# Second product's results added to the rows by accumulating transfers issued from GpSimd, in seven of eight blocks

## The chip, the cores and the metric

The kernel runs on one NeuronCore of a Trainium2 chip. The metric is the device time of one execution in microseconds (us), the median over runs. A core has a matrix engine (TensorE, PE in the profile), three other compute engines (VectorE = DVE, ScalarE = ACT, GpSimd = POOL), a queue engine (SyncE = SP) that issues most transfers, and 16 DMA engines that carry them. Each engine works through its own queue in order and waits on semaphores for the others.

## The reference

```python
def _attn_ref(q, k, v, omega):            # (8, 8, 576, 64), omega (128, 64)
    ...
    q_p, k_p = (phi(q_s), phi(k_s))       # exp features, 128 per head
    kv = np.einsum('bhsm,bhsd->bhmd', k_p, v)
    z = np.sum(k_p, axis=2)
    num = np.einsum('bhsm,bhmd->bhsd', q_p, kv)
    den = np.einsum('bhsm,bhm->bhs', q_p, z)[..., None] + 1e-06
    return (num / den).astype(np.float32)

def _moe_ref(x, w_ch1, w_ch2):            # x: (8, 576, 512), weights 512x2048 and 2048x512
    X = np.fft.fft(x, axis=1)
    X = np.fft.fft(X, axis=2)
    u = x + np.real(X).astype(np.float32)
    mu = np.mean(u, axis=-1, keepdims=True)
    var = np.mean((u - mu) ** 2, axis=-1, keepdims=True)
    un = (u - mu) / np.sqrt(var + 1e-06)
    ch = np.maximum(un @ w_ch1, 0.0) @ w_ch2
    return (u + ch).astype(np.float32)
```

`reference` runs the first, puts its heads side by side (8 x 576 rows of 512), and runs the second on that. All in float32.

## The kernel before

There are 8 x 576 = 4608 rows of 512. A first stage (to about 424 us) computes attention and the Fourier mix and writes the rows `u` to DRAM (`us`); it also does the two-layer network for the first 512 rows in a plain way. The second stage takes the other 4096 rows in eight blocks of 512 (`NTB` = 8, `j` = 0 to 7). This is where the change lies.

In each block both matrix products of the network are done by a fast scheme: each operand is cut into 2 x 2 parts, seven products of sums of parts are formed instead of eight, and the results are added together.

- **First product**, `first_of(j, fc)`: eight chunks `fc` of the hidden width. TensorE multiplies (L1310), ScalarE and VectorE evict with the relu into `hid` (L1296, L1324, L1362), and GpSimd forms four sums of parts per chunk, into `hs` and `hid` (L1377).
- **Second product**, `product_of(j, i, cells)`: seven products in the order 1, 2, 4, 5, 6, 7, 3 (`ORDER`). Products 1, 2, 4 and 7 read `hid`; 5, 6 and 3 read `hs`. Each product is itself done by the same scheme, as seven *leaves* of four matmuls (L1490). A leaf reads one tile `wl` of the second weight, 256 KB, loaded by SyncE from DRAM (L1393) into one of 12 buffers. Sums of the left factor come from VectorE (L1457). The leaves are evicted by ScalarE to `s` (L1465) and by VectorE with an add into `part` (L1470: c11, c12, c22); the last leaf's quarter is copied into `part` by ScalarE (L1523).

`part` holds one product's result: 128 partitions of 2 x 256 floats, 256 KB. There are four such buffers. The block's rows are in two cells `cells[0]` and `cells[1]` (tiles `ur2`, three buffers, loaded from `us`, L948), each of two row tiles of 512 columns; `cell(t, m)` is the half `m` of the columns of cell `t`. Each product's `part` is added into one or two of these halves: product 1 into (0,0), 2 into (0,0), 4 into (1,0), 5 into (0,1) and (1,1), 6 into (0,1), 7 into (1,1) and (1,0), 3 into (0,1). Before 6 and 7 add, the `part` of 6 and then that of 7 are added to the kept `part` of product 1 (`cells["u"]`), and that buffer is what is added; it is released after product 7, the others after their own last add. The function `plus` makes such an add, on GpSimd or VectorE, whichever would end earlier by the planner (L1530). When all adds of a cell are done, SyncE stores it (`stored`, L954).

The order of everything is set when the program is built: the class `Listing` takes streams of `Step`s, each with an engine, an assumed duration, the events it waits for and the buffers it takes and gives, and always issues the step that could begin first by its own clock. In the second stage there is no list of fixed picks, so a change of any step's assumed cost can move the order on every engine. Each engine then runs its list in order; tile dependences become semaphore waits.

The last product of the last block has its own ending (`ends`).

Of the kernel before, what the change touches and what calls it, by code (L numbers as in the profile page):

```python
# [15 lines left out]
ALU = mybir.AluOpType  # L16
# [19 lines left out]
PE, ACT, DVE, POOL, SP, NONE = "pe", "act", "dve", "pool", "sp", "none"  # L36
# [244 lines left out]
def kernel(  # L281
# [10 lines left out]
    nc = tc.nc  # L292
# [30 lines left out]
    NTB = (B * S - NPLAIN * TP) // TB  # L323
# [152 lines left out]
    us = dram.tile([B * S, DM], F32, name="us")  # L476
# [954 lines left out]
    def product_of(j, i, cells):  # L1431
# [10 lines left out]
        part = late.tile([128, 2, HM], F32, name="part", tag="part", bufs=4)  # L1442
# [83 lines left out]
        def plus(o, other, **kw):  # L1526
            step = Step({POOL: 1.35, DVE: 0.7}, port=True, **kw, bias=0.06)
            yield step
            eng = nc.gpsimd if step.eng == POOL else nc.vector
            eng.tensor_tensor(out=o, in0=o, in1=other, op=ALU.add)  # L1530

        def cell(t, m):
            return cells[t][:, :, HM * m : HM * m + HM]

        def done(n):
            return (("second", j, n), "done")

        us = tuple(("ur2", j, t) for t in range(2))
        if i in (1, 6, 7):
# [4 lines left out]
            part, give = cells["u"], ("part",) if i == 7 else ()  # L1544
        else:
            to = {2: ((0, 0),), 4: ((1, 0),), 5: ((0, 1), (1, 1)), 3: ((0, 1),)}[i]
            give = ("part",)
        for n, (t, m) in enumerate(to):
            last = n == len(to) - 1
            yield from plus(  # L1550
                cell(t, m), part[:], after=(us[t],), give=give if last else (),
                makes=done(i) if last else None,
            )

    def second_of(j, cells):
        t0 = (NPLAIN * TP + TB * j) // 128
# [25 lines left out]
    def halves():  # L1582
        for j in range(NTB):
            for fc in range(HF):
                yield Step(NONE, take=("set", "ht", "ht"))
                yield Fork(first_of(j, fc))
            cells = {}
            yield Fork(second_of(j, cells))
            for i in ORDER:
                yield Step(NONE, take=("set",))  # L1590
                yield Fork(product_of(j, i, cells))
# [40 lines left out]
```

## Time and profile before

| | |
|---|---|
| median of 3 runs | 1170.17 us (1165.61 to 1170.54) |
| profiled execution, from first to last instruction | 1172.2 us |
| granted TensorE clock, mean | 0.996 of full speed |
| second stage | from 424 us to the end |
| L1470 in the second stage (VectorE) | 168 instructions, 49.0 us |
| L1523 in the second stage (ScalarE) | 55 instructions, 15.3 us |
| L1530 into the cells, on VectorE | 39 instructions, 26.8 us |
| L1530 into the kept `part`, on VectorE | 16 instructions, 11.0 us |
| DMA queue of SyncE | 166576 packets, 218.09 MB |

How to read it: the profile is of one execution, which took 1172.2 us; all durations are from it. Busy time is the time in which an engine executed; instructions that only issue a transfer or wait are not counted. A row of a group reads: line, engine, operation, output <- inputs, count, then busy time and mean duration in ns, then the idle time of the engine just before these instructions and what ended it. The chain of waits is followed back from the last instruction: each piece is either work on an engine, or the time from the issue of a transfer to its arrival. In tables of stretches, each engine's busy time stands with its instruction count, then the granted TensorE clock, the busy share of the 16 DMA engines, and GB/s.

### The profile page before, as it was taken

How to read it: one execution, taken by the hardware profiler on the slowest of the kernel's cores; microseconds unless marked ns; L12 is line 12 of the kernel's file. 1: busy time of each engine (PE TensorE's matmuls, PEld its weight loads, DVE VectorE, ACT ScalarE, POOL GpSimd, SP SyncE). 2: the span in 40 equal slices, each digit the busy share in tenths (PEclk: the TensorE clock that was granted, in tenths of full speed). 3: DMA queues.
4: the chain of work that ended last, by engine and by line, in shares of the span. 5: the costliest groups of instructions: out<-in, count | busy, mean ns of one | idle time of the engine just before them, and what ended most of it. 6: DMA issues, size and time to landing. Idle time of an engine off the chain costs nothing.

```text
span 1172.2 us, 31328 instructions
## 1 busy us (share of the span) xinstructions
PE 1153.5 (98%) x12437; PEld 1032.9 (88%) x12437; DVE 754.7 (64%) x1573; ACT 436.8 (37%) x1485; POOL 430.4 (37%) x496
## 2 busy tenths in 40 slices
PE   8999999999999999999999999999999999999998
PEld 7888888779777868998998998898999899899898
DVE  5999999986676655744754664573573574474255
ACT  6998898866444212122112212212212212221211
POOL 2433444455472106225225324413513512522421
PEclk8999999999999999999999999999999999999999
DMA  7866765665662254873783593694495396388055
GB/s 218 224 188 186 240 181 178 203 210 163 207 196 101 77 162 139 263 264 85 222 278 112 172 308 99 152 317 141 112 319 190 82 290 231 83 258 263 35 166 203
DMA packets 167217, 220.34 MB, mean 188 GB/s; under 512 B 50080, under 2 KB 81056, under 8 KB 167072
## 3 DMA queue, kind: packets, MB, share of 16 engines
q1 hardware_dynamic: 166576, 218.09, 60.7%
q8 instruction: 98, 1.61, 0.6%
q14 instruction: 47, 0.39, 0.1%
q10 hardware_dynamic: 496, 0.26, 0.1%
HBM read 179.24 MB, written 43.25 MB: 190 GB/s over the span
## 4 chain that ended last, share of the span: by engine, by line
PE 88%; DMA 5%; DVE 4%; ACT 2%; SPq 1%; issue 1%; DVEq 0%
PE banks L1310 33%; PE banks L1490 27%; PE banks L1099 5%; PE banks L606 5%; PE banks L1122 4%; PE banks L512 4%; DMA wl<-w2l 3%; PE banks L640 2%; PE banks L687 2%; PE banks L849 2%; PE banks L799 1%; ACT e L566 1%; DVE nmx L549 1%; DMA kq<-in_k_dram 1%; PE banks L809 1%; PE banks L860 1%
## 5 line engine op out<-in xcount | busy, mean ns | idle before, releaser
L1490 PE MATMUL banks<-wl,sums 128*128 128x128 f32 x1792 | 217.4, 275 | 0.0
L1490 PEld LDWEIGHTS banks<-wl,sums 128*128 128x128 f32 x1792 | 208.6, 192 | 0.0
L1296 DVE CUSTOM_DVE_ANT_0 hid<-banks,s 128x256 f32<-128x256 f32 x192 | 80.9, 424 | 188.8 <-PE banks L1310 188.8
L566 ACT ACTIVATE e<-banks,nmx 128x128 f32<-128x128 f32 x576 | 165.3, 434 | 23.2 <-DVE nmx L549 22.4
L1324 ACT ACTIVATE s<-banks 128x256 f32<-128x256 f32 x192 | 73.7, 384 | 259.0 <-PE banks L1310 259.0
L1310 PE MATMUL banks<-unT,w 128*128 128x256 f32 x704 | 166.3, 379 | 0.0
L1310 PEld LDWEIGHTS banks<-unT,w 128*128 128x128 f32 x704 | 133.2, 190 | 18.3 <-issue 0.5
L1530 POOL TENSOR_TENSOR ur<-ur,part 128x512 f32<-128x512 f32 x32 | 47.3, 1479 | 267.1 <-ACT part L1523 187.0
L1465 ACT ACTIVATE s<-banks 128x128 f32<-128x128 f32 x168 | 46.6, 278 | 256.7 <-PE banks L1490 220.3
L1310 PE MATMUL banks<-tt,w1s 128*128 128x256 f32 x512 | 126.3, 379 | 0.0
L1310 PEld LDWEIGHTS banks<-tt,w1s 128*128 128x128 f32 x512 | 97.0, 190 | 13.7 <-DVE hid L1296 0.4
L1490 PE MATMUL banks<-wl,hid 128*128 128x128 f32 x768 | 100.0, 276 | 3.2 <-DMA wl<-w2l 3.1
L1470 DVE TENSOR_TENSOR part<-banks,s 128x128 f32<-128x128 f32 x168 | 49.0, 292 | 83.4 <-PE banks L1490 82.2
L549 DVE TENSOR_REDUCE nmx<-banks 128x8 f32<-128x1024 f32 (+1 forms) x96 | 89.3, 951 | 19.7 <-PE banks L606 15.5
L1490 PEld LDWEIGHTS banks<-wl,hid 128*128 128x128 f32 x768 | 94.0, 192 | 6.0 <-DMA wl<-w2l 4.5
L606 PE MATMUL banks<-om,kqT 64*64 64x128 f32 (+1 forms) x2088 | 80.6, 278 | 1.9 <-ACT kv L656 1.2
L1310 PE MATMUL banks<-unT,w1s 128*128 128x256 f32 x320 | 79.5, 379 | 0.0
L606 PEld LDWEIGHTS banks<-om,kqT 64*64 64x64 f32 (+1 forms) x2088 | 65.8, 140 | 13.3 <-issue 4.3
L1490 PE MATMUL banks<-wl,hs 128*128 128x128 f32 x576 | 75.1, 275 | 0.5 <-DVE part L1470 0.4
L1490 PEld LDWEIGHTS banks<-wl,hs 128*128 128x128 f32 x576 | 70.1, 192 | 1.2 <-DVE part L1470 0.6
L1377 POOL TENSOR_TENSOR hs<-hid,hs 128x256 f32<-128x256 f32 x64 | 50.1, 784 | 57.2 <-issue 37.1
L1310 PEld LDWEIGHTS banks<-unT,w1s 128*128 128x128 f32 x320 | 60.4, 190 | 8.7
(128 smaller groups left out, 1914.6 us busy)
## 6 DMA issues: line engine op xcount, KB each, us to landing
wl<-w2l SPq DMA_DIRECT2D x392, 256.0 KB
raw<-in_moe_w_ch_dram SPq DMA_DIRECT2D x32, 512.0 KB
kq<-in_k_dram SPq DMA_DIRECT2D x32, 288.0 KB
kq<-in_q_dram SPq DMA_DIRECT2D x32, 288.0 KB
vd<-in_v_dram SPq DMA_DIRECT2D x32, 288.0 KB
u<-us SPq DMA_DIRECT2D x36, 256.0 KB
ur<-us SPq DMA_DIRECT2D x36, 256.0 KB
out_dram<-ur SPq DMA_DIRECT2D x34, 256.0 KB
```

Source lines behind the costliest of these rows:

```text
L512: nc.tensor.transpose(ps[:, (j - j0) * 128 : (j - j0 + 1) * 128], src(j), ident[:])
L549: nc.vector.tensor_reduce(nmx[:, :, 0:num], pps[:, :, 0 : MF * num].rearrange("p b (c m) -> p b c m", m=MF), axis=AX.X, op=ALU.max, negate ...
L566: nc.scalar.activation(out=e[:, c + (i if num == 1 else 0), :], in_=pps[:, i, MF * c : MF * c + MF], func=AF.Exp, bias=nmx[:, i, c : c + 1],)
L606: nc.tensor.matmul(pps[cols, c, MF * m : MF * m + MF], lhsT=kqT[rows, j, cols], rhs=om2[rows, :],)
L1099: nc.tensor.matmul(hp[:, 0:TP], lhsT=w1[:, dc, 128 * fc : 128 * fc + 128], rhs=unTs[key][:, dc, :], start=(dc == 0), stop=(dc == NDC - 1),)
L1296: nc.vector._custom_dve(TENSOR_ADD_SAT, out=o, in0=ps, in1=sb, s0=FMAX, s1=0.0)
L1310: nc.tensor.matmul(ps[:, 0:HT].rearrange("f (b q) -> f b q", q=Q), lhsT=left(dc), rhs=right(dc), start=start and dc == 0, stop=(dc == D2 - 1),
L1324: nc.scalar.activation(out=s[:], in_=ps[:, 0:HT], func=AF.Copy)
L1377: nc.gpsimd.tensor_tensor(out=o, in0=l, in1=r, op=op)
L1470: nc.vector.tensor_tensor(out=part[:, t, 128 * m : 128 * m + 128], in0=ps[:, 0:128], in1=saved[with_][:], op=ALU.add,)
L1490: nc.tensor.matmul(ps[:, 0:128], lhsT=left[:, f], rhs=wls[j, i, n][:, f], start=start and f == 0, stop=(f == 3), skip_group_check=True,)
L1530: eng.tensor_tensor(out=o, in0=o, in1=other, op=ALU.add)
```

## The change

In blocks 0 to 6 the add of `part` into a cell is no longer an instruction of VectorE or GpSimd: GpSimd issues a transfer from `part` to the cell which adds what it carries to what lies there. The planner is told 1.0 us on GpSimd, 4.0 us until it is in, and the load of 100 KB on the transfers. The sums of `part` into `cells["u"]` stay as they were, and in block 7 the adds stay on the engines.

```diff
         for n, (t, m) in enumerate(to):
             last = n == len(to) - 1
-            yield from plus(
-                cell(t, m), part[:], after=(us[t],), give=give if last else (),
-                makes=done(i) if last else None,
-            )
+            how = dict(after=(us[t],), give=give if last else (), makes=done(i) if last else None)
+            if j == NTB - 1:
+                yield from plus(cell(t, m), part[:], **how)
+                continue
+            yield Step(POOL, 1.0, 4.0, kb=100, **how)
+            nc.gpsimd.dma_start(cell(t, m), part[:], accum_op=ALU.add)
```

## The prediction

> **What bounds the kernel now.** I read the page first, then TensorE's waits in the second stage (420 to 1172 us), then the chain that ended last, then the DMA share in short stretches.
>
> ```profile
> span 1172.2 us, 31328 instructions
> ...
> PE 1153.5 (98%) x12437; PEld 1032.9 (88%) x12437; DVE 754.7 (64%) x1573; ACT 436.8 (37%) x1485; POOL 430.4 (37%) x496
> ...
> L1530 POOL TENSOR_TENSOR ur<-ur,part 128x512 f32<-128x512 f32 x32 | 47.3, 1479 | 267.1 <-ACT part L1523 187.0
> ...
> wl<-w2l SPq DMA_DIRECT2D x392, 256.0 KB
> ```
>
> ```profile
> PE banks L1490 <- DMA wl<-w2l: 3.1, 5, 1.4
> PE banks L1490 <- DVE part L1470: 0.4, 1, 0.4
> ```
>
> TensorE is busy 98% of the span, and those two lines are all that it waits for in the second stage: 3.5 us. The changed adds (L1530) are named in neither. So nothing that only frees VectorE or GpSimd can pay. The chain gives the ceiling of a gain and the weak spot:
>
> ```profile
> 482.18 6.71 DMA wl<-w2l
> ...
> 570.94 5.40 DMA wl<-w2l
> ...
> 701.15 5.18 PE banks L1310 x24
> ...
> 753.66 5.73 DMA wl<-w2l
> ...
> 794.55 5.18 PE banks L1310 x24
> ...
> 847.06 4.96 DMA wl<-w2l
> ...
> 939.78 6.12 DMA wl<-w2l
> ...
> 1035.99 5.69 DMA wl<-w2l
> ```
>
> The piece L1310 x24 comes once a block, at 516.06, 608.81, 701.15, 794.55, 887.27, 981.11 and 1074.15, so the blocks last 92.75, 92.34, 93.40, 92.72, 93.84 and 93.04 us. Six blocks exceed the shortest by 4.1 us together: that is what the transfers of `wl` cost now, and about the most that any edit of other engines could win. The six DMA pieces are loads of 256 KB on loaded engines, from issue to the matmul that they release: 34.6 / 6 = 5.77 us on average. How loaded the engines are (the last two columns are DMA share and GB/s):
>
> ```profile
> 745.40:745.90 0.50, 0.50 (x4) 0.45 (x3) 0.28 (x1) 0.00 (x0) 0.50 (x2) 1.00 0.83 176
> 745.90:746.40 0.50, 0.50 (x4) 0.42 (x4) 0.50 (x1) 0.25 (x1) 0.42 (x2) 1.00 0.84 315
> 746.40:746.90 0.50, 0.50 (x4) 0.45 (x3) 0.47 (x2) 0.13 (x1) 0.50 (x1) 1.00 0.06 21
> ...
> 860.00:864.00 4.00, 4.00 (x39) 4.00 (x38) 2.86 (x6) 0.55 (x2) 0.00 (x0) 1.00 1.05 387
> ...
> 880.00:884.00 4.00, 4.00 (x39) 4.00 (x38) 1.14 (x4) 0.50 (x2) 1.27 (x1) 1.00 0.90 287
> ```
>
> The first three show one load alone, issued at 744.41: its bytes move until 746.4 and it is in by 746.9, 2.5 us after issue. During a block's products the engines run at 82 to 108%, up to 387 GB/s; at TensorE's own pace (one leaf of 256 KB in 0.89 us) they need 287 to 294.
>
> **The change, part by part.** Removed in blocks 0 to 6: nine adds into the cells per block, 63 in all: by the counts in both programs 28 on GpSimd (28 x 1.479 = 41 us) and 35 on VectorE (35 x 0.685 = 24 us). TensorE waited 0.4 us for VectorE and never for GpSimd: worth 0 to 0.4 us, I take 0. The two sums of `part` per block stay on VectorE, and block 7 keeps its adds.
>
> Added: 63 transfers of 256 KB, 16.5 MB more on engines that carried 220 MB. Each is cut into 256 pieces of 1 KB, since a cell's row is two runs of 256 floats, and must read the cell besides the source. GpSimd issues them in its one queue. By the order in the changed program, between the last chunk's sums and the next block's first: the add for product 1, the last two sums of chunk 7 (L1377), then 2, 4, 5, 5, 6, 7, 7, one sum of the next block, 3. Those L1377 sums behind product 1's transfer feed products 7 and 3, some 14 us later; the others feed the next block's products, over 40 us later: nothing. On SP the stores L954 now wait for transfers instead of adds, and one is moved behind two loads of `u`. Behind the store stand `wl` loads, but they run 12 leaves ahead, into the next block, with 40 us of L1310 between: nothing as long as a transfer lands within that.
>
> Moved on TensorE: the leaves of products 5, 6, 7 and 3 are interleaved otherwise; the same 3136 records of L1490 at 0.89 us per eight, so 0 us by themselves.
>
> The wait that counts is the buffer `part`. There are four. Product 1's is held until 7 is done; 2, 4 and 5 take the other three; product 6 needs the one that product 2's transfer has read. That transfer waits for product 1's (same half of the same cell), which waits for product 1's last copy. So two transfers in series must fit between product 1's last leaf and product 6's second leaf, when VectorE writes `part` (L1470). In the changed order 16 leaves lie between (13 before): 16 x 0.892 = 14.3 us. Product 1's copy ends 0.6 us after its leaf (leaf to 856.6, L1523 856.93 + 0.28), so 13.7 us are left, 6.85 per transfer from GpSimd's issue to landing. If it is longer, L1470 stands at the head of VectorE's queue with the sums (L1457) of product 7 behind it, TensorE gets no bank back, and each block loses 2 x (L - 6.85).
>
> No row shows a transfer that GpSimd issues, nor one that adds; L is bounded by rows. From below: the lone load, 2.5 us: two links take 5, nothing is lost. From above: a loaded load, 5.77; plus a dearer issue: SP takes 0.56 us for one of 512 pieces (L980), and the same add takes GpSimd 1.8 us at worst for VectorE's 0.685, a factor 2.6, so 1.5 us in place of SP's 0.35, +1.1; plus the second read, 256 KB at 387 GB/s, +0.7. L = 7.6. I take 7.6: the transfers fall into the stretch where the engines run at 82 to 108%, nearer to the six pieces than to the lone load. Loss: 2 x (7.6 - 6.85) = 1.5 us per block, 7 blocks, 10.5 us. Against the execution of 1172.2 us that is 1182.7; the median shown (1170.17) lies 2.0 lower, so I predict 1181.
>
> The Trainium skill, "DMA: Bandwidth & Descriptors", section "Anatomy of one DMA — SWDGE (gpsimd) path", puts a GpSimd-issued transfer at about 2.0 us plus its bytes over 436 GB/s. By it L would be 2.6 us, an estimate, and the sum 1170. The lone load of 2.5 us agrees with it, the six loaded ones of 5.0 to 6.7 don't. The same page, section "SWDGE vs HWDGE vs iDMA", has each engine alternate between the queues; no row here shows two queues at once.
>
> **The rivals.** (a) Hidden: L stays under 6.85. For it: the lone load; a block's products take 44 us for nine transfers; TensorE has 12 leaves (10.7 us) of loads in hand. Against: shares above 1. Time 1170 (1172.2 less 2.0).
> (b) Starved: adding costs the engines far more than one copy and the `wl` loads come late. A plain copy of 256 KB is 0.68 us of all engines. Cover per block: from product 1's end 27 us at (387 - 294) / 387 = 24% spare, 6.5 us, and 10.7 us in hand less 2.5 to 3 for landing, 7.9: 14.4 us. Nine transfers at 2 x 0.68 are 12.2, just covered; at 3 x, 18.4, lost 4.0 x 7 = 28 us; at 4 x, 24.5, lost 71 us. Time 1198 to 1241, middle 1215. For it: small pieces and double reads. Against: a 1 KB piece is large beside the 512 B ones of L980.
> (c) Faster: the four us of `wl` waits go, because stretches at a block's start empty out: 1166. It decides only if the fetches of `unT` leave the front of product 1's loads; in SP's changed order they stand where they stood, which speaks against it.
>
> **How the numbers follow.** Forecast (late links) 0.40, own range 1174 to 1196 (L from 7.1 to 8.7); (a) 0.36; (b) 0.16; (c) and small gains like it 0.08. About 0.5% (5.9 us) is what can be told from no change here. (c) ends right at that bound, so half of it counts as faster, 0.04; the other half and (a) make 0.40; forecast and (b) 0.56 slower. The range goes from (c) to the lower part of (b): 1166 to 1212.
>
> **What would show it.** Right: VectorE's L1470 waiting once a block for a transfer into `ur`, TensorE's wait of 1 to 3 us at products 6 or 7, blocks of 94 to 95 us. Rival (a): blocks of 92.3 to 93.8 and TensorE's waits still near 3.5 us. Rival (b): waits for `wl` grow in the middle of the products, at DMA shares above 1. The forecast is wrong if a transfer lands in under 6 us, or if the engines need more than twice a copy's time for it.

## The result, and the profile after

| | before | after |
|---|---|---|
| median | 1168.79 us (4 runs, 1165.61 to 1170.54) | 1181.74 us (4 runs, 1179.39 to 1183.54) |
| ratio to before | | 1.0114, 95% interval 1.0093 to 1.0136 |
| profiled execution | 1172.2 us | 1181.8 us |
| second stage, first to last matmul | 743.75 us | 754.83 us |

The kernel is slower by 1.1%, 13 us. The profiled execution of the kernel before was a long one: every other profiled execution here was timed at 1.7 to 2.9 us more than its span, so a span of 1172.2 stands for some 1174 (an estimate), above all four timed runs. A gap in that trace counts for that execution and not for the median. The page of the kernel after (span; busy time by engine; the transfer queue of GpSimd with packets, MB and share of the engines' time; the group of the new transfers; their time from issue to landing):

```profile
span 1181.8 us, 31420 instructions
...
PE 1155.9 (98%) x12437; PEld 1031.6 (87%) x12437; DVE 745.0 (63%) x1538; ACT 437.4 (37%) x1485; POOL 460.1 (39%) x531
...
q0 software_dynamic: 17136, 16.52, 9.0%
...
L1555 POOL DMA_DIRECT2D ur<-part x63 | 76.6, 1358 | 280.2 <-ACT part L1523 100.6
...
ur<-part POOLq DMA_DIRECT2D x63, 256.0 KB, 8.3
```

VectorE does 35 instructions less, as the diff says. GpSimd is not relieved: its 63 issues keep it busy for 76.6 us, more than the 28 adds that it no longer does. TensorE has the same 12437 matmuls. What TensorE waits for in the second stage (us in total, times, longest):

```profile
PE banks L1490 <- ACT s L1465: 3.2, 4, 1.1
PE banks L1490 <- issue: 2.3, 3, 1.8
PE banks L1490 <- DMA wl<-w2l: 1.8, 5, 0.7
PE banks L1310 <- DVE hid L1296: 1.5, 6, 0.3
PE banks L1490 <- DVE part L1470: 0.4, 1, 0.4
```

Before, two rows stood here, loads of `wl` with 3.1 us and L1470 with 0.4. The loads have fallen to 1.8; the first, second and fourth row are new. The names of the releasers hide the cause, though. A bank that comes back late is put down to the last semaphore, here ScalarE's eviction or "issue", and short gaps are not listed at all. So I summed the gaps from the start times of all 4928 matmul records of the stage: the distance to the next start less the pace (0.2159 us for L1310, 0.1117 us for L1490), put down to the leaf before which it stands or in which it lies; gaps of under 0.02 us are left out. The leaves are named by their number in the fast scheme, as the products are; a product's leaves come in the order 1, 2, 5, 6, 3, 7, 4, and leaf 3 reads the fourth sum.

```
gaps of TensorE in the second stage, us     before   after    difference
product 6, leaf 3                             -       6.8       +6.8
first product (L1310)                        0.3      3.5       +3.2
product 4, leaf 3                             -       1.8       +1.8
product 7, leaf 3                             -       1.2       +1.2
product 4, leaves 1 and 2 (wl)               5.6      4.0       -1.6
product 5, leaf 1                            0.4       -        -0.4
product 3, leaf 4                            0.6      0.6        0.0
all                                          6.9     18.0      +11.1
```

These 11.1 us are the whole growth of the stage (754.83 - 743.75). The chain has the piece L1310 x24 once a block again; four of its seven:

```profile
702.72 5.18 PE banks L1310 x24
...
798.56 5.18 PE banks L1310 x24
...
892.40 5.18 PE banks L1310 x24
...
987.28 5.18 PE banks L1310 x24
```

The blocks between them last 95.84, 93.84 and 94.88 us; all six average 94.63, against 93.02 before.

**The two transfers in series.** One block in the timeline (start, length, engine, line, operation; in brackets the idle time before it and what ended it), first GpSimd, VectorE and TensorE about product 6:

```profile
863.55 1.22 POOL L1555 DMA_DIRECT2D ur<-part  x1 [11.53 <-ACT part L1523]
...
871.69 2.43 POOL L1555 DMA_DIRECT2D ur<-part  x2 [4.95 <-ACT s L1465]
...
878.50 0.29 DVE L1470 TENSOR_TENSOR part<-banks,s 128x128 f32<-128x128 f32 x1 [1.47 <-DMA ur<-part]
878.71 0.68 DVE L1457 TENSOR_TENSOR sums<-hs,sums 128x512 f32<-128x512 f32 x1
879.49 1.69 PE L1490 MATMUL banks<-wl,sums 128*128 128x128 f32 x13 [0.25 <-issue]
```

Product 1's transfer is issued at 863.55 and lands 7.57 us later, at 871.13; product 2's goes out 0.56 us after that, at 871.69, and lands 6.69 us later, at 878.37. At 878.50 VectorE writes the buffer, then forms the sum behind it, the fourth of product 6, and at 879.49 TensorE begins leaf 3, which reads that sum.

**The pile behind product 3's transfer.** Some 28 us later, in the same block:

```profile
906.92 1.20 POOL L1555 DMA_DIRECT2D ur<-part  x1 [5.69 <-DVE rstd L1024]
...
907.69 1.18 POOL L1377 TENSOR_TENSOR hs<-hs,hid 128x256 f32<-128x256 f32 x1
...
909.06 1.00 POOL L1026 TENSOR_TENSOR rstd<-rstd,mhalf 128x1 f32<-128x1 f32 x1
...
910.10 3.65 DVE L1028 TENSOR_SCALAR u<-u,mv,rstd 128x512 f32<-128x512 f32 x1 [3.22 <-POOL rstd L1026]
...
912.34 1.12 POOL L1377 TENSOR_TENSOR hs<-hid,hs 128x256 f32<-128x256 f32 x1
...
914.43 1.05 DVE L1296 CUSTOM_DVE_ANT_0 hid<-banks,s 128x256 f32<-128x256 f32 x3
...
915.20 1.13 PE L1310 MATMUL banks<-tt,w 128*128 128x256 f32 x4 [0.26 <-DVE hid L1296]
```

GpSimd stands 5.69 us before it can issue the transfer for product 3. The sums of the next block's first chunks, which lie behind it, then run back to back until 913.46: the last five begin 0.68 to 0.69 us apart and their records last 1.12 to 1.15 us, so each begins before the one ahead of it has ended. In that run VectorE's L1028, which takes 0.94 us elsewhere, takes 3.65 and ends at 913.75; the evictions L1296 come late, and TensorE waits for them. All instances of L1028 (ns: shortest, median, longest), first after, then before:

```profile
L1028 DVE TENSOR_SCALAR u<-u,mv,rstd x36: 536/940/3662, 101.9 to 1034.0; 128x512 f32<-128x512 f32 x36
```

```profile
L1028 DVE TENSOR_SCALAR u<-u,mv,rstd x36: 533/939/1486, 103.5 to 1025.6; 128x512 f32<-128x512 f32 x36
```

### The profile page after: what moved, and what is told of

It reads as the page before. It is cut to its first block, busy times and chain, and to the rows that moved or that the text cites. A ratio compares the mean times of both kernels' runs of the same rounds, so it can differ in the third digit from the quotient of the medians.

```text
span 1181.8 us, 31420 instructions
## 1 busy us (share of the span) xinstructions
PE 1155.9 (98%) x12437; PEld 1031.6 (87%) x12437; DVE 745.0 (63%) x1538; ACT 437.4 (37%) x1485; POOL 460.1 (39%) x531
## 4 chain that ended last, share of the span: by engine, by line
PE 81%; DMA 6%; DVE 6%; issue 2%; ACT 2%; POOL 1%; SPq 1%; POOLq 0%; DVEq 0%; ACTq 0%
PE banks L1310 27%; PE banks L1490 26%; PE banks L1099 5%; PE banks L606 5%; PE banks L512 4%; PE banks L1122 4%; DMA wl<-w2l 3%; PE banks L640 2%; DVE u L1028 2%; PE banks L687 2%; PE banks L849 2%; DMA raw<-in_moe_w_ch_dram 1%; PE banks L799 1%; DMA u<-us 1%; PE banks L809 1%
## 5 line engine op out<-in xcount | busy, mean ns | idle before, releaser
L1490 PE MATMUL banks<-wl,sums 128*128 128x128 f32 x1792 | 217.3, 276 | 5.5 <-ACT s L1465 3.2
L1490 PEld LDWEIGHTS banks<-wl,sums 128*128 128x128 f32 x1792 | 208.5, 192 | 8.6 <-ACT s L1465 3.8
L1555 POOL DMA_DIRECT2D ur<-part x63 | 76.6, 1358 | 280.2 <-ACT part L1523 100.6
L1296 DVE CUSTOM_DVE_ANT_0 hid<-banks,s 128x256 f32<-128x256 f32 x192 | 78.2, 420 | 148.2 <-PE banks L1310 148.2
L1310 PE MATMUL banks<-unT,w 128*128 128x256 f32 x704 | 167.5, 379 | 0.0
L1310 PEld LDWEIGHTS banks<-unT,w 128*128 128x128 f32 x704 | 132.7, 190 | 17.9 <-issue 0.5
L1470 DVE TENSOR_TENSOR part<-banks,s 128x128 f32<-128x128 f32 x168 | 48.9, 291 | 137.7 <-PE banks L1490 117.8
L1310 PE MATMUL banks<-tt,w1s 128*128 128x256 f32 x512 | 124.2, 379 | 0.1
L1310 PEld LDWEIGHTS banks<-tt,w1s 128*128 128x128 f32 x512 | 96.7, 190 | 14.1 <-DVE hid L1296 0.5
L549 DVE TENSOR_REDUCE nmx<-banks 128x8 f32<-128x1024 f32 (+1 forms) x96 | 89.4, 951 | 20.3 <-PE banks L606 15.2
L1490 PE MATMUL banks<-wl,hid 128*128 128x128 f32 x768 | 99.8, 276 | 1.9 <-DMA wl<-w2l 1.8
L1490 PEld LDWEIGHTS banks<-wl,hid 128*128 128x128 f32 x768 | 94.1, 192 | 4.6 <-DMA wl<-w2l 3.3
L1310 PE MATMUL banks<-unT,w1s 128*128 128x256 f32 x320 | 80.6, 379 | 0.0
L1490 PE MATMUL banks<-wl,hs 128*128 128x128 f32 x576 | 73.9, 275 | 0.4 <-DVE part L1470 0.4
L1490 PEld LDWEIGHTS banks<-wl,hs 128*128 128x128 f32 x576 | 69.5, 192 | 0.9 <-DVE part L1470 0.6
L1028 DVE TENSOR_SCALAR u<-u,mv,rstd 128x512 f32<-128x512 f32 x36 | 47.9, 1330 | 34.7 <-POOL rstd L1026 34.7
L1310 PEld LDWEIGHTS banks<-unT,w1s 128*128 128x128 f32 x320 | 60.8, 190 | 8.3
```

The lines of the kernel that those rows point to most:

```text
L549: nc.vector.tensor_reduce(nmx[:, :, 0:num], pps[:, :, 0 : MF * num].rearrange("p b (c m) -> p b c m", m=MF), axis=AX.X, op=ALU.max, negate ...
L1028: nc.vector.tensor_scalar(u[:], u[:], mv[:, 0:1], rstd[:], op0=ALU.subtract, op1=ALU.mult)
L1296: nc.vector._custom_dve(TENSOR_ADD_SAT, out=o, in0=ps, in1=sb, s0=FMAX, s1=0.0)
L1310: nc.tensor.matmul(ps[:, 0:HT].rearrange("f (b q) -> f b q", q=Q), lhsT=left(dc), rhs=right(dc), start=start and dc == 0, stop=(dc == D2 - 1),
L1470: nc.vector.tensor_tensor(out=part[:, t, 128 * m : 128 * m + 128], in0=ps[:, 0:128], in1=saved[with_][:], op=ALU.add,)
L1490: nc.tensor.matmul(ps[:, 0:128], lhsT=left[:, f], rhs=wls[j, i, n][:, f], start=start and f == 0, stop=(f == 3), skip_group_check=True,)
```

## The experiments

The theory had three terms: the two transfers in series, the pile behind product 3's transfer, and the new order of the instructions in itself. The edits of the A series are to the kernel after, those of the B series to the kernel before. Times and ratios are against runs of the kernel before on the same chip (its median lay between 1166.9 and 1170.2 us).

### A6: the new order alone

The transfers are left out and nothing is put in their place, so blocks 0 to 6 lack the second product in their rows. What is left is the order that the planner made for the change.

```diff
-            nc.gpsimd.dma_start(cell(t, m), part[:], accum_op=ALU.add)
```

> The changed kernel's order with the 63 transfers left out and nothing in their place, so the rows of blocks 0 to 6 lack the second product. Theory (the denser order alone makes TensorE wait for the sums of VectorE, some 0.6 us a block): 1171 to 1175, and 3 to 5 us above the kernel before without its adds. Rival (the order costs nothing by itself): the same as that kernel, within 1.5 us.

Measured: 1169.74 us (1167.74 to 1171.01), ratio 1.0018 (1.0004 to 1.0031). The gaps sum to 6.7 us, 1.2 of them at product 6 and 1.2 at product 7, 0.4 in the first product. The time lies below the expected 1171 to 1175, on a chip where the kernel before took 1166.9.

### B2: the old order without the adds

The 63 adds into the cells are left out, in the order of before; blocks 0 to 6 lack the second product in their rows here too.

```diff
+            if kw.get('after') and kw['after'][0][0] == 'ur2' and j < NTB - 1:
+                return
```

> The kernel before in its own order, with its 63 adds of blocks 0 to 6 into the cells left out, so the rows of these blocks lack the second product. It is what the removal alone is worth. Theory (adds off the path): 1167 to 1171, as before within 0.3%. Rival (the adds on VectorE and GpSimd held TensorE up): below 1166.

Measured: 1165.82 us (1164.83 to 1169.12), ratio 0.9997 (0.9988 to 1.0006). Nothing at products 6 and 7. The time falls below 1166, as the rival had it, but on this chip the kernel before took 1166.9, so the ratio decides. So the removed adds were worth nothing that can be told: taking them away altogether gains at most 0.1% (1.4 us of 1169). And the order alone costs 1.0018 less 0.9997, some 2.4 us, as much as the two gaps of 1.2 together (the two medians differ by 3.9, and the intervals of the ratios just touch, so it is the gaps that carry this). They come to 0.17 us in each block. In the new order leaf 3 of products 6 and 7 comes just two leaves after leaf 5, and the fourth sum, which leaf 3 reads, goes into the tile that leaf 5 has read, so TensorE waits a moment for it.

### A1: the same order, with the adds on GpSimd

```diff
-            nc.gpsimd.dma_start(cell(t, m), part[:], accum_op=ALU.add)
+            nc.gpsimd.tensor_tensor(out=cell(t, m), in0=cell(t, m), in1=part[:], op=ALU.add)
```

> The changed kernel's order on every engine is kept, with each of the 63 transfers replaced by the same add as an instruction of GpSimd (1.27 to 1.5 us) at the same place of its queue. Theory (the transfers' lateness costs, not the new order): time like before, 1166 to 1171, no wait of TensorE behind a reused buffer of part. Rival (the planner's new order costs): 1176 to 1182, as the changed kernel.

Measured: 1183.06 us (1181.95 to 1186.33), ratio 1.0109 (1.0088 to 1.0129), gaps 20.1 us, 8.0 of them at product 6 and 3.4 at product 2's last leaf. As slow as the change and slower than either expectation, though no transfer is left to be late. But it is no clean test: GpSimd's adds have a cost of their own, which shows in this kernel's timeline:

```profile
874.60 2.49 POOL L1555 TENSOR_TENSOR ur<-ur,part 128x512 f32<-128x512 f32 x2 [3.20 <-ACT part L1523]
...
875.97 1.66 DVE L1457 TENSOR_TENSOR sums<-hs,sums 128x512 f32<-128x512 f32 x1 [0.50 <-PE banks L1490]
...
877.73 2.02 PE L1490 MATMUL banks<-wl,sums 128*128 128x128 f32 x16 [0.91 <-ACT s L1465]
```

While GpSimd makes two adds in 2.49 us, VectorE's sum (0.69 us in most places) takes 1.66 and ends at 877.63, and TensorE, which needs it, goes on at 877.73 after 0.91 us. What follows is only that in this order GpSimd is no better place for the adds than the transfers. With A6 it tells that equal times can have two causes: had I stopped here, I would have blamed the order. One thing more is in this trace. GpSimd waits for product 3 here too, and the same sums pile up behind that add and run back to back from 906.29 on; yet L1028 takes 0.94 us among them, at 908.25, and the gaps of the first product come to 0.2 us.

### A2: a fifth buffer for `part`

The room comes from moving `ur1` to another pool; the planner still counts with four, so the order stays.

```diff
-    ur1 = const.tile([128, DM], F32, name="ur1")
...
+    ur1 = fix.tile([128, DM], F32, name="ur1")
...
-        part = late.tile([128, 2, HM], F32, name="part", tag="part", bufs=4)
+        part = late.tile([128, 2, HM], F32, name="part", tag="part", bufs=5)
```

> The changed kernel with a fifth buffer of part; the planner still counts four, so the order stays. (Room for it comes from ur1, which moves from the constants to the first stage's pool.) Then product 6 no longer waits for product 2's transfer, product 7 does, 6 us later. Theory (two transfers in series before product 6 cost about 1 us a block): the wait goes, 1174 to 1177. Rival (the DMA engines or the piled GpSimd queue cost it): 1180 to 1183.

Measured: 1178.8 us (1176.21 to 1182.56), ratio 1.0071 (1.005 to 1.0092). The gap at product 6 falls from 6.8 to 1.2, the price of the order, while the landings stay as long as they were:

```profile
DMA to landing us min/median/max: 3.8/8.1/12.3
```

So the buffer was what made product 6 wait. The time lies between the two expected ranges. The ratio falls by 0.0043, 5.0 us; the gap alone saves 5.6, and against that stands one new gap of 2.0 us at the start of the stage, from the move of `ur1` (B3 has it too). So gaps and times agree only within the interval of the ratio.

### A10: transfers of half the bytes

The same number of pieces, 512 B instead of 1 KB; half of each result is not added to the rows.

```diff
-            nc.gpsimd.dma_start(cell(t, m), part[:], accum_op=ALU.add)
+            nc.gpsimd.dma_start(cell(t, m)[:, :, 0:128], part[:, :, 0:128], accum_op=ALU.add)
```

> The same 63 transfers with half the bytes: the same number of pieces, 512 B each, so half of each result is not added. Theory (a transfer's engine time goes with its bytes, twice over): engine time 1.7 to about 1.0 us, issue to landing 8.3 to 6.5 to 7.5 us, the two links then fit 14.3 us nearly and the wait at product 6 falls from 6.8 to 1 to 3 us: a ratio of 1.005 to 1.008. Rival (the number of pieces sets it): landing stays at 8 us or more, 1.010 to 1.012.

Measured: 1174.96 us (1173.08 to 1180.27), ratio 1.0054 (1.0034 to 1.0073). The landings and the queue's share of the engines:

```profile
DMA to landing us min/median/max: 3.1/6.5/10.7
```

```profile
q0 software_dynamic: 17136, 8.26, 5.8%
```

The wait at product 6 is gone (1.3 us left), the pile is not (3.4 us in the first product). With the traces of the change and of A3 below, this gives the wait as a function of the two landings. For each block, the time from issue to landing of product 1's and of product 2's transfer together, and the gap just before the leaf:

```
sum of both landings, us -> gap before the leaf, us (blocks 0 to 6)
change  15.30 1.16   14.55 0.69   13.66 0.10   15.79 1.94   14.26 0.41   15.13 1.29   14.20 0.68
A3      13.25 0.10   15.47 1.68   15.93 2.13   14.87 1.08   14.33 0.53   15.73 1.93   14.81 1.02
A10     14.33 0.19   12.74 0.10   12.76 0.10   13.63 0.10   12.93 0.10   11.45 0.10   10.93 0.10
```

Below 13.9 the gap is 0.10, which is the order's; above, it grows one for one with the sum: 0.1 + (sum - 13.9) fits 12 of the 14 blocks of the first two rows within 0.06, and the other two (blocks 0 and 6 of the change) within 0.35. Block 0 of A10 lies off it as block 0 of the change does: 14.33 with a gap of 0.19, 0.34 less than the line.

### A4: the same transfers without the add

A plain copy; the cells of blocks 0 to 6 are overwritten instead of added to, so the sums are left out.

```diff
-            nc.gpsimd.dma_start(cell(t, m), part[:], accum_op=ALU.add)
+            nc.gpsimd.dma_start(cell(t, m), part[:])
```

> The same transfers, order and waits, but they copy instead of adding, so the rows get the last part alone: the output leaves the sums out. Theory (reading the cell as well makes the transfer long): issue to landing falls from 8.3 to 5 or 6 us, engine time of a transfer from 1.7 to 0.7 to 1.0 us, 1172 to 1177. Rival (the issue by GpSimd and the shared engines make it long, not the add): landing stays at 7 to 8.5 us, 1179 to 1183.

Measured: 1177.68 us (1175.89 to 1180.83), ratio 1.0067 (1.0047 to 1.0088), just above the expected 1172 to 1177. Landings and queue:

```profile
DMA to landing us min/median/max: 2.7/5.4/7.9
```

```profile
q0 software_dynamic: 5040, 16.52, 3.8%
```

The same bytes come in 63 x 80 packets instead of 63 x 272, and take 3.8% of the engines instead of 9.0%. The wait at product 6 is gone, and so are the gaps of the first product; but a new one of 7.1 us stands at product 2's last leaf. In its timeline:

```profile
857.33 2.49 DVE L1171 TENSOR_TENSOR unT<-unT 128x512 f32<-128x512 f32 x1
...
857.84 0.74 POOL L1377 TENSOR_TENSOR hid<-hid 128x256 f32<-128x256 f32 x1
```

A sum of VectorE (0.68 us in the kernel before, 1.21 in the change) takes 2.49 while GpSimd's issue and two sums, now at another time, go past it. So the ratio of A4 is no price of the add: one collision of the two engines went and another came.

The collision that went tells something about the pile. Behind product 3's copy the same sums pile up and run back to back (GpSimd and VectorE):

```profile
901.10 0.72 POOL L1555 DMA_DIRECT2D ur<-part  x1 [5.68 <-DVE rstd L1024]
...
903.74 0.72 POOL L1377 TENSOR_TENSOR hs<-hid 128x256 f32<-128x256 f32 x1
903.80 0.99 DVE L1028 TENSOR_SCALAR u<-u,mv,rstd 128x512 f32<-128x512 f32 x1 [2.74 <-POOL rstd L1026]
904.43 0.94 POOL L1377 TENSOR_TENSOR hs<-hid,hs 128x256 f32<-128x256 f32 x1
```

L1028 takes 0.99 us in the middle of them, and TensorE loses nothing. The sums last 0.71 to 0.74 us here, but for the one beside L1028, and hardly overlap. So the pile alone, here and in A1, does not keep VectorE out; it did so in each trace where the transfer ahead of it was an adding one (the change, A2, A9, A10, A11: 3.66 to 3.93 us at the longest).

### A3: product 3's add on VectorE

```diff
+            if i == 3:
+                nc.vector.tensor_tensor(out=cell(t, m), in0=cell(t, m), in1=part[:], op=ALU.add)
+                continue
             nc.gpsimd.dma_start(cell(t, m), part[:], accum_op=ALU.add)
```

> The changed kernel in the same order, but product 3's add is an instruction of VectorE instead of a transfer, so that GpSimd's sums of the next block's first chunk no longer stand behind a transfer that waits for product 3. Theory (that wait piles up GpSimd's queue, and L1028 on VectorE then takes 3.66 us beside it): L1028 back to about 0.94 us in all cases, TensorE's waits for L1296 gone, 1177 to 1180. Rival (L1028 costs nothing on TensorE's path): 1181 to 1183.

Measured: 1181.61 us (1177.63 to 1184.24), ratio 1.0088 (1.0067 to 1.011). The gaps in the first product fall from 3.5 to 0.6, and no L1028 is long any more:

```profile
L1028 DVE TENSOR_SCALAR u<-u,mv,rstd x36: 539/939/1489, 101.4 to 1034.7; 128x512 f32<-128x512 f32 x36
```

The ratio's step against the change, 0.0026 or 3.0 us, is that of the gaps, but the intervals overlap, and the time itself lies in the rival's range (1181 to 1183) and not in the theory's. And the profiled execution was not shorter (1182.5 us): at product 6 it waited 9.0 us instead of 6.8. The table under A10 says why: in this execution the two landings summed to 14.91 us a block instead of 14.70, which on the rising part of the curve is more wait. What it left open, A12 was for.

### A11: L1028 in another form

In blocks 1 to 7 the same computation is written as an instruction with two tensor operands, at a line of its own, L1029.

```diff
-        nc.vector.tensor_scalar(u[:], u[:], mv[:, 0:1], rstd[:], op0=ALU.subtract, op1=ALU.mult)
+        if block:
+            nc.vector.scalar_tensor_tensor(u[:], u[:], mv[:, 0:1], rstd[:].to_broadcast([P, DM]), op0=ALU.subtract, op1=ALU.mult)
+        else:
+            nc.vector.tensor_scalar(u[:], u[:], mv[:, 0:1], rstd[:], op0=ALU.subtract, op1=ALU.mult)
```

> The changed kernel, transfers and order kept; in blocks 1 to 7 VectorE's L1028 does the same arithmetic as an instruction with two scalars' places filled by a scalar and a broadcast column (scalar_tensor_tensor). Theory (L1028 in its first form waits until GpSimd's run of sums ends; another form gets in between): no instance above 2 us, TensorE's wait at the first chunks falls from 3.5 to under 1 us, a ratio of 1.007 to 1.009. Rival (VectorE waits for GpSimd in any form, or L1028 is not what holds TensorE): 3 us and more stay, 1.010 to 1.012.

Measured: 1183.65 us (1180.33 to 1187.25), ratio 1.0122 (1.0103 to 1.0142). The new form waits just as long beside GpSimd's run:

```profile
911.78 3.92 DVE L1029 SCALAR_TENSOR_TENSOR u<-u,mv,rstd 128x512 f32<-128x512 f32 x1 [3.22 <-POOL rstd L1026]
```

The theory that another form would get in between GpSimd's instructions fell. The form makes no difference to the wait; it lasts until GpSimd's run behind the adding transfer is over.

### A9 and A8: product 1 on VectorE, then 1 and 3

A9 takes one link out of the series; A8 takes out the pile besides, with 49 transfers left.

```diff
+            if i == 1:
+                nc.vector.tensor_tensor(out=cell(t, m), in0=cell(t, m), in1=part[:], op=ALU.add)
+                continue
```

```diff
+            if i in (1, 3):
+                nc.vector.tensor_tensor(out=cell(t, m), in0=cell(t, m), in1=part[:], op=ALU.add)
+                continue
```

> The changed kernel in the same order, with product 1's add alone on VectorE: one transfer, not two in series, before product 6. Product 3's stays a transfer. Theory (terms add up): the wait at product 6 falls to the 1.2 us of the order, the pile behind product 3's transfer stays at 3 us and L1028 at 3.66 us once a block: 5 to 6 us above the kernel before, a ratio of 1.004 to 1.006. Rival (the loss moves, as it did when product 3's add was taken out alone): 1.008 or more.

> The changed kernel in the same order, with the adds of products 1 and 3 as instructions of VectorE and the other 49 transfers kept. Product 2's transfer then has no transfer ahead of it, and no sum of GpSimd stands behind one that waits for product 3. Theory (three terms: two transfers in series 5.6 us, the pile behind product 3's transfer 3.2 us, and the denser order of the leaves 4 us; only the last is left): 1171 to 1175. Rival (49 transfers load the engines and the loss moves elsewhere, as product 3's did when it alone was taken out): 1178 to 1182.

Measured: A9 1174.2 us (1171.97 to 1175.61), ratio 1.0045 (1.0032 to 1.0059): product 6 at 1.2, the first product still at 4.0, where TensorE's waits in that trace name the same releaser as before:

```profile
PE banks L1310 <- DVE hid L1296: 2.1, 7, 0.6
```

A8 1168.95 us (1166.49 to 1172.76), ratio 1.0021 (1.001 to 1.0033), within the intervals the same as the order alone (A6, 1.0018): 49 accumulating transfers then cost nothing that can be told. More had been expected, 1171 to 1175, since the order had been put at 4 us where it costs 2.4. In both the gap at product 4's leaf 3 is gone too. Two of GpSimd's sums (L1377) stand behind product 1's transfer; in the changed kernel they run beside a sum of VectorE (L1457), which then takes 1.21 us for its 0.68 (at 866.08), and TensorE loses 0.15 us there in each block, 0.45 in the first.

### A12: the fifth buffer, and product 3 on VectorE

The diffs of A2 and A3 together.

> The fifth buffer of part and, besides, product 3's add done by VectorE; everything else as in the changed kernel. Theory (the pile of sums behind product 3's transfer has a price of its own, about 3 us, apart from the two transfers in series): with the fifth buffer alone the ratio was 1.0071; now the first product's gaps fall from 5.3 to about 2 us (2.0 of it is the one gap that moving ur1 makes), the gap at product 6's leaf stays at 1.2, and the ratio falls by 0.0028 to 1.0035 to 1.0050. Rival (moving product 3 only shifts the lateness to another place, as the longer wait at product 6 in the profile with product 3 alone suggests): the ratio stays within 0.001 of 1.0071, and a new gap of about 3 us in sum shows at products 6, 7 or 3.

Measured: 1175.34 us (1169.93 to 1180.29), ratio 1.0046 (1.0028 to 1.0064). The gap at product 6 is 1.2, the first product's gaps are 2.2 (2.0 of it is the gap that the move of `ur1` makes), L1028 is never longer than 1.49 us, and no new gap has come. Against A2 the ratio falls by 0.0025, 2.9 us, as the theory had it. The two intervals overlap, so it is the gaps that speak against the rival, by which the lateness only moves to another place.

### B3: before, with one more buffer for `wl`

To see whether the kernel before has anything to win at its `wl` waits, it gets a 13th buffer.

```diff
-                    wl = late.tile([128, 4, 128], F32, name="wl", tag="wl", bufs=NWL)
+                    wl = late.tile([128, 4, 128], F32, name="wl", tag="wl", bufs=NWL + 1)
```

The room comes from `ur1` as in A2.

> The kernel before in its own order, with a 13th buffer of wl (room from ur1, which moves to the first stage's pool). TensorE's only waits in the second stage there are 5.6 us at product 4's first two leaves, whose loads queue behind the fetches of unT. Theory (one leaf more in hand takes 0.9 us off each such wait): 2 to 4 us less, 1165 to 1168. Rival (the engines are full there, and what is in hand is used up the same): 1168 to 1171.

Measured: 1166.27 us (1164.04 to 1170.26), ratio 0.9997 (0.9987 to 1.0007). The waits for `wl` are gone, and the one gap of 2.1 us from the move of `ur1` has come; the time is the same, where 2 to 4 us less had been expected. No kernel run here beats the one before by an amount that can be told.

## Why the prediction was right, and where it was not

The forecast of late links came true: 1181 was predicted, 1181.74 measured. But the sum fits better than its terms, and that it came so close is luck. Of the 10.5 us that it put on the two transfers in series, 5.6 are there; the rest is work that it priced at nothing. The step from the profile to the median was too small by some 1.7 us as well, an estimate: it set a span of 1172.2 us beside a timed median, while that execution, timed, would have been some 1174.

1. **The removed adds, 0 to 0.4 us, taken as 0.** Right: without them and with nothing in their place the old order runs at 0.9997 (B2).
2. **The two transfers in series: the place was right, the limit nearly, the size was not.** The wait stands at product 6, and VectorE's L1470 waits there for a transfer into `ur`. The forecast gave the pair 13.7 us, and by the table under A10 the wait begins at 13.9. What is behind L1470 in VectorE's queue is not product 7's sums but product 6's own fourth, one leaf earlier than thought. That the limit fits so well is partly luck. The prediction had VectorE late as soon as product 6's second leaf is done, at 877.29 in the block shown; by the gap there, L1470 could have begun as late as about 878.2 without loss (an estimate: 878.50 less the 0.31 us by which the gap exceeds 0.10). It also had nothing between the first landing and the second issue, where 0.56 to 0.57 us go by in six of the seven blocks. The two nearly cancel. Each of three ways to break the series (A2, A9, A10) brings the gap from 6.8 to 1.2 or 1.3 us.

   The mis-sized term is L. It was taken as 7.6 us, and the two links measured 7.92 and 6.78, 7.35 on average. A difference of 0.25 us is little in L and much in the loss, which is twice what L exceeds 6.85 by: by the measured sum and limit it is 14.7 - 13.9 = 0.8 us a block, which is what the gaps show (5.6 / 7), against 1.5 predicted. L's own parts were off by more, in opposite directions. A4's copies in the same two places landed in 6.47 and 4.57 us, 5.52 on average, where the prediction had 5.77 + 1.1 = 6.9 before the second read; the adding transfers then took 1.8 us more than the copies, where it had 0.7. The median of all 63, 8.3 us, is not the series' number: of the pairs issued right behind each other at products 5 and 7, the second landed in 10.4 and 10.0 us on average.
3. **The sums behind product 3's transfer, "nothing".** This step failed. The prediction asked when their results are needed (over 40 us later, true) and not what they do when they all run at once. GpSimd idles for product 3, works off the pile without a pause, and VectorE's L1028 does not get through until the run ends. It costs 3.2 us in the gaps; in time, 3.0 us (change to A3), 2.9 us (A2 to A12) and 2.8 us (A9 to A8), each with intervals that overlap. These steps take the pile and the adding issue ahead of it away together. A1 and A4 part the two: behind an add and behind a copy the same pile let L1028 through in 0.94 and 0.99 us, so the pile alone costs nothing. What sets the change apart is the adding issue ahead of the pile, after which each sum's record overlaps the next (GpSimd's spans in a profile are rough, VectorE's 3.66 us do not rest on them).

   The Trainium skill has a rule for this in "SBUF — State Buffer", section "🔬 SBUF: two separate sides": VectorE and GpSimd share a pair of ports as an exclusive lock, and whichever of certain instructions starts first keeps the other out for its whole length. The trace agrees that VectorE is kept out, 3.66 us for 0.94. But it was kept out for more than one instruction: four more of GpSimd's sums began while the L1028 shown was under way, and a form with two tensor operands waited as long (3.92, A11).
4. **The sums behind product 1's transfer, "nothing".** Small but not nothing: 1.8 us in the gaps at product 4's leaf 3. It is 1.8 to 2.1 us in every trace where GpSimd issues product 1's adding transfer or makes that add itself (the change, A1, A2, A3, A10, A11, A12), 0.2 with A4's copies, and absent where GpSimd has nothing to do for product 1 (A6, A8, A9). It was not isolated further.
5. **The leaves in another order, "0 us by themselves".** Failed by 2.4 us. The count of matmuls is the same, but two leaves now come sooner than VectorE's sums for them (A6 against B2). The prediction weighed only whether a leaf has a `wl` tile and its place in the queue, not the sums of the left factor.
6. **Loads of `wl`, rivals (b) and (c).** Their waits fell by 1.6 us, perhaps because TensorE, held up elsewhere, leaves the loads more time; that is argued, not shown. The old order had 1.9 us of them in B2's trace, so the 5.6 of before may belong to that one execution. Rival (b), starved engines, had its condition met and its price not: the adding transfers took 9.0% of 1181.8 us, 1.69 us of all 16 engines each, against 0.71 for the copies of A4 (3.8% of 1174.1 us, over 63), 2.4 times a copy. Nine of them are 15.2 us a block, over the rival's cover of 14.4, so by it some 0.8 x 7 = 5.6 us should have gone to late loads. Nothing shows them, and A8, with 49 such transfers, waits for `wl` less than before (1.8 us in its gaps, 5.6 before): the cover was sized too small. The prediction called itself wrong at more than twice a copy's time; that test was badly chosen. So was the other one, a landing in under 6 us: product 3's transfers landed in 4.6 us on average, the two in series in 6.45 to 8.67. Rival (c) had the four us of `wl` waits as its gain. B3 takes these waits away altogether and is no faster, though it pays 2.1 us for the move of `ur1`.
7. **The stores on SP.** Nothing is seen of them, as said.
8. **Rival (a), hidden,** needed L under 6.85. A10 shows it from the other side: where the pair lands within 13.9 us the series costs nothing, and the order and the pile remain. The 2.6 us that the prediction worked out from the Trainium skill ("DMA: Bandwidth & Descriptors", section "Anatomy of one DMA — SWDGE (gpsimd) path") and set against its own 7.6 is under every landing here: the shortest of the 63 took 3.8, the shortest of A4's copies 2.7.

The terms again, from the gaps: 5.6 + 3.2 + 2.4 + 1.8 - 1.6 = 11.4 us, less 0.4 for a gap of before that has gone, is, but for rounding, the 11.1 by which the stage grew; 1.3 us came off before the stage in this execution. In ratios the same goes step by step: the change 1.0114, without product 1's link 1.0045, without product 3's too 1.0021, the order alone 1.0018, the old order 0.9997.

What stays open: why in A1 the same adds by GpSimd cost so nearly what the transfers cost (its 8.0 us at product 6 have another cause, seen in the timeline but not taken apart), and why GpSimd's sums overlap behind an adding issue, and keep VectorE out until they end, but not behind a copy or an add.

## What to carry to other kernels

Work moved to a transfer is not gone: its source buffer is held until the landing, so count the buffers, and put every pair of transfers that the next use must wait for, one after the other, against the time that there is; where the two are within a few per cent of each other, rows of other transfers can bound the loss but not size it. When an engine's queue gets an instruction that waits, ask not only when what stands behind it is needed but what it will run beside when it is let go all at once; and vary what stands ahead of the pile, for the same pile cost 3 us behind an adding transfer and nothing behind a copy or an add. And price a planner's new order as a part of the change: run it without the work it was made for.

## What the runs showed of the hardware that was not expected

- **An adding transfer is cut smaller and costs more than a copy of the same tile.** 256 KB took 256 packets of 1 KB and some, 1.69 us of all engines, 1.20 us of GpSimd to issue and a median of 8.3 us to land; the copy took 64 of 4 KB and some, 0.71 us, 0.72 us and 5.4 us. So the layout of the cell's rows, which the prediction gave as the reason for the 1 KB pieces, is not the reason: it is the same for the copy. On an engine a 1 KB piece of the adding kind took 105 ns, a copied 4 KB piece 177. The Trainium skill, "Collectives: The Full Stack", section "The bandwidth ceiling: the fold count and why AG ≠ RS ≠ AR", lays the halved rate of a reducing transfer to its two source reads, not to the add. The factor of 2.4 here is no contradiction, but pieces of different size are in it. A10's adding pieces of 512 B took 67 ns, so along a straight line one of 4 KB would take some 336 ns, 1.9 times the copied one: an estimate, drawn well beyond the sizes that were measured.
- **Half the bytes in the same number of pieces land only a little sooner:** 6.5 us for 8.3 (A10), with 5.8% of the engines for 9.0%. Along a straight line, which is an estimate, 3.6 of the 8.3 us go with the bytes and more than half does not.
- **Beside GpSimd, single instructions of VectorE take two to four times as long:** L1028 0.94 to 3.66 us (the change), L1171 0.68 to 2.49 (A4), L1457 0.69 to 1.66 (A1), each beside several instructions of GpSimd in a row. In the pile of the change GpSimd loses nothing by it: the last five records are 1.12 to 1.15 us long instead of 0.72, but they begin 0.68 to 0.69 us apart, as they do elsewhere. Behind product 1's transfer, where VectorE's instructions get in between, GpSimd is held up too: two sums begin 1.23 us apart (864.35 and 865.58).
- **An adding issue leaves its mark on what GpSimd does next:** behind it the sums' records overlap and VectorE's L1028 waits for the end of the run; behind a copying issue (A4) or an add (A1) the same run leaves L1028 at 0.94 to 0.99 us. What in the issue does this stays open.
